# Attention and two feed-forward layers on one core: softmax's division moved behind the product, the norm's Newton steps per token, and row loads on another queue

## The chip, the cores and the metric

The program runs on one core of a Trainium2 chip. A time is the device time of one execution in microseconds; the kernel before took 961.56 us (median of three runs, 961.1 to 962.03). The profile is of one further execution of 961.0 us. In it PE is TensorE's matmuls, PEld its weight loads, DVE VectorE, ACT ScalarE, POOL GpSimd and SP the SyncE, whose queue issues nearly all DMAs.

## What is computed

The reference is a causal attention with a decay, followed by two feed-forward layers. Between the two layers, and at the end, nothing is summed over tokens, so tokens can be worked on in blocks.

```python
scores = scale * np.matmul(q, k.transpose(0, 1, 3, 2))      # batch 4, 8 heads, 576 tokens, 64 wide
cum = np.cumsum(np.log(np.clip(f, 0.0001, 1.0)), axis=-1)
scores = np.where(causal, -1000000000.0, scores + (cum[:, :, :, None] - cum[:, :, None, :]))
attn = np.exp(scores - np.max(scores, axis=-1, keepdims=True))
attn = attn / (np.sum(attn, axis=-1, keepdims=True) + 1e-09)
x = np.matmul(attn, v)                    # heads side by side: 2304 tokens x 512
y = ((x @ w1) * (x @ w2)) @ w3 @ w_out    # 512 -> 1024 -> 1024 -> 512
xn = y / np.sqrt(np.mean(y * y, axis=-1, keepdims=True) + 1e-06) * rms_g
out = (silu(xn @ w_gate) * (xn @ w_val)) @ moe2_w_out       # 512 -> 1536 -> 512
```

## The kernel before

**Attention.** 32 heads are worked on one after the other, two of them (a pair) side by side in the 128 partitions of `X`. For a head, `attn_s` multiplies queries and keys into PSUM in five blocks of query rows (`QB`; 64, 128, 128, 128 and 128 rows), `row_max` takes each block through DVE (mask, maximum, copy into `PB`), and `row_exp` makes the exponentials on ACT, with their row sums in `rsum`. `attn_t` transposes the probabilities on PE, splits them into a high part `PTh` (ACT) and a low part `PTl` (DVE), and `pv` multiplies both with the values; its last step adds the two halves into `X` (L541). The decay enters as extra rows of the product: four rows of `rq`/`rk` or `Q2`/`K2` hold 8 times the cumulated logarithm `cum` in two parts, and ones.

**Division.** For the first two pairs (heads 0 to 3) the probabilities stay undivided; `rcol`, the reciprocals of the pair spread over the columns, is transposed on PE and multiplied onto `X` (`normalize`, L543 to L556). From head 4 (`LATE`) on, `attn_s` adds 1e-9 to the five row sums, takes the reciprocals into `rinv` (L468, L469) and scales each of the five blocks of `PB` with them, on whichever of ACT, DVE and POOL is planned free first (L470 to L473).

**Rows.** `cum` of all heads is written to DRAM once (`cq_d`, `cn_d`); each later head loads its two pairs of rows from there into `Q2` and `K2` (L398, L399), issued from ACT's queue through `send`. Head 0's rows are made by DVE and ACT (L1073, L1075), head 1's by two DMAs on ACT's queue (L1083, L1084).

**First layer.** Tokens go in six blocks of 384 (`bk`). `ab_group` makes the two products of a block, L691 multiplies them, `y_group` multiplies by the product of w3 and w_out that was made beside attention (L647). `norm` then sums the squares over channels on PE with a matrix of ones, which leaves the sum in all 128 partitions, and takes the inverse root on 128x384 by a bit trick and three Newton steps (L727 to L733; the squares on ACT). The result is scaled into `yn_d`. `norm` of a block stands after the second pair of groups of the next one.

**Second layer.** Its products go through sums of weight pieces. `widen` loads a piece (1 MB), repairs its bits (L571 to L574), combines parts (L770) and stores it (`sw_d`, `wo_d`). `EARLY` = 12 pieces are planned into the first half (`raw_w`), six behind it (`xf`). `gate` (L872) and `wout` (L953) follow as one dense row of matmuls, three times.

**What sets the order.** All instructions are given to `Plan` with their durations and dependences; `begins` works out when each must start, and `order` then writes one list for each engine, in which an instruction that may run on several engines goes to the one that is planned to finish it first. Every engine runs its list in order, and SP and ACT wait in order before they issue a DMA. First-layer blocks serve as filler for PE during attention. The lines below are the functions that the change touches and what calls them.

Of the kernel before, what the change touches and what calls it, by code (L numbers as in the profile page):

```python
# [39 lines left out]
EARLY = 12  # L40
# [4 lines left out]
FROWS = D + 4  # L45
LATE = 4
# [37 lines left out]
class Plan:  # L84
# [37 lines left out]
    def begins(self):  # L122
# [4 lines left out]
        for i in range(len(ops) - 1, -1, -1):  # L127
# [12 lines left out]
    def order(self):  # L140
# [27 lines left out]
        while len(out) < n:  # L168
# [48 lines left out]
def body(ctx, tc, q, k, v, f, w12, w3, wo1, wgv, wo2, g, out):  # L217
# [166 lines left out]
    def prep(h, at):  # L384
        p = h % 2
        if h < NQ:

# [831 lines left out]
```

## Time and profile before

| | |
|---|---|
| median of three runs | 961.56 us (961.1 to 962.03) |
| the profiled execution | 961.0 us, span 959.2 us |
| PE, PEld busy | 938.5 us (98 %), 893.6 us (93 %) |
| DVE busy | 844.1 us (88 %) |
| ACT, POOL busy | 549.4 us (57 %), 231.7 us (24 %) |
| DMA on SP's and ACT's queue | 154.02 MB, 0.58 MB |
| chain that ended last | PE 63 %, DVE 27 %, issue 4 %, DMA 3 % |

A matmul counts as busy until its last result is out, and the next one begins before that; so a busy PE can still be waiting, and the weight loads (PEld) show it better. The shares are means over the whole program, whose parts have different limits; the windows below part them.

### The profile page before, as it was taken

How to read it: one execution, taken by the hardware profiler on the slowest of the kernel's cores; microseconds unless marked ns; L12 is line 12 of the kernel's file. 1: busy time of each engine (PE TensorE's matmuls, PEld its weight loads, DVE VectorE, ACT ScalarE, POOL GpSimd, SP SyncE). 2: the span in 40 equal slices, each digit the busy share in tenths (PEclk: the TensorE clock that was granted, in tenths of full speed). 3: DMA queues.
4: the chain of work that ended last, by engine and by line, in shares of the span. 5: the costliest groups of instructions: out<-in, count | busy, mean ns of one | idle time of the engine just before them, and what ended most of it. 6: DMA issues, size and time to landing. Idle time of an engine off the chain costs nothing.

```text
span 959.2 us, 15426 instructions
## 1 busy us (share of the span) xinstructions
PE 938.5 (98%) x5480; PEld 893.6 (93%) x5480; DVE 844.1 (88%) x1553; ACT 549.4 (57%) x1132; POOL 231.7 (24%) x242
## 2 busy tenths in 40 slices
PE   7999999999999999999999999999999999999998
PEld 4687889899899999899999999999999999999998
DVE  6999999999999999866666659999988899988896
ACT  4888888777776667543333244546444456454442
POOL 2145437264444442401102022015000012000000
PEclk9999999999999999999999999999999999999999
DMA  7764564645444733354864223632663334643322
GB/s 250 206 205 149 162 227 143 213 142 194 163 135 161 247 135 109 129 202 160 321 243 154 94 97 123 236 138 67 191 242 116 111 99 146 214 151 116 132 66 99
DMA packets 43868, 155.58 MB, mean 162 GB/s; under 512 B 4880, under 2 KB 20496, under 8 KB 37136
## 3 DMA queue, kind: packets, MB, share of 16 engines
q1 hardware_dynamic: 43448, 154.02, 47.4%
q8 instruction: 43, 0.70, 0.3%
q10 hardware_dynamic: 344, 0.58, 0.2%
q14 instruction: 33, 0.27, 0.1%
HBM read 124.13 MB, written 30.44 MB: 161 GB/s over the span
## 4 chain that ended last, share of the span: by engine, by line
PE 63%; DVE 27%; issue 4%; DMA 3%; ACT 2%; POOL 1%; ACTq 0%; DVEq 0%; POOLq 0%
PE bank L872 27%; PE bank L684 13%; PE bank L953 8%; PE bank L708 6%; DVE PTl L497 3%; PE wide L953 3%; DVE qk L251 3%; DVE wbig L251 1%; DVE x L541 1%; PE bank L490 1%; DVE raw_w L574 1%; PE wide L530 1%; DVE lbig L251 1%; DVE raw_w L770 1%; DVE PB4b L433 1%
## 5 line engine op out<-in xcount | busy, mean ns | idle before, releaser
L684 PE MATMUL bank<-xhl,wbig 128*128 128x384 f32 x1152 | 216.9, 338 | 0.1
L684 PEld LDWEIGHTS bank<-xhl,wbig 128*128 128x128 f32 x1152 | 198.2, 188 | 1.9 <-DVE wbig L251 0.5
L872 PE MATMUL bank<-xop,wbig 128*128 128x384 f32 x1008 | 182.6, 336 | 0.8 <-ACT cs L894 0.8
L872 PEld LDWEIGHTS bank<-xop,wbig 128*128 128x128 f32 x1008 | 175.3, 188 | 1.4 <-ACT cs L894 1.1
L872 PE MATMUL bank<-xop,lbig 128*128 128x384 f32 x504 | 95.0, 336 | 0.0
L872 PEld LDWEIGHTS bank<-xop,lbig 128*128 128x128 f32 x504 | 88.0, 188 | 0.0
L497 DVE TENSOR_TENSOR PTl<-bank,PTh 128x512 fp32r<-128x512 f32 (+3 forms) x116 | 64.6, 580 | 3.9 <-ACT PTh L496 3.5
L708 PE MATMUL bank<-uh,Wch 128*128 128x384 f32 x192 | 65.0, 339 | 0.0
L708 PE MATMUL bank<-uh,Wcl 128*128 128x384 f32 x192 | 64.4, 335 | 0.0
L708 PE MATMUL bank<-ul,Wch 128*128 128x384 f32 x192 | 64.3, 335 | 0.0
L496 ACT CAST PTh<-bank 128x512 fp32r<-128x512 f32 (+3 forms) x116 | 54.5, 506 | 11.6 <-PE bank L490 10.6
L647 PE MATMUL bank<-wbig,w 128*128 128x512 f32 x192 | 54.3, 407 | 0.0
L692 ACT CAST uh<-u 128x384 fp32r<-128x384 f32 x48 | 24.6, 514 | 43.3 <-DVE u L691 43.0
L260 POOL TENSOR_SCALAR qk<-rq 64x576 fp32r<-64x576 f32 x42 | 32.1, 769 | 58.9 <-PE wide L416 52.1
L530 PE MATMUL wide<-PTh,V 128*128 128x512 f32 (+4 forms) x145 | 45.0, 317 | 1.3 <-DVE nmaxb L433 1.1
L530 PE MATMUL wide<-PTl,V 128*128 128x512 f32 (+4 forms) x145 | 44.6, 332 | 1.0 <-DVE PTl L497 0.9
L691 DVE TENSOR_TENSOR u<-bank,a 128x384 f32<-128x384 f32 x48 | 26.4, 551 | 21.3 <-PE bank L684 21.0
L251 DVE TENSOR_TENSOR lbig<-zf,lbig 128x768 fp32r<-128x768 f32 x46 | 44.7, 978 | 0.2
L878 DVE TENSOR_TENSOR zf<-cs 128x384 f32<-128x384 f32 x72 | 39.9, 555 | 4.7 <-ACT cs L883 2.9
L251 DVE TENSOR_TENSOR wbig<-nrm,wbig 128x768 fp32r<-128x768 f32 (+1 forms) x41 | 42.9, 1047 | 0.4 <-ACT wbig L258 0.3
L258 ACT ACTIVATE lbig<-zf 128x768 fp32r<-128x768 f32 x32 | 27.2, 849 | 25.9 <-PE bank L953 9.6
L953 PE MATMUL bank<-lbig,wbig 128*128 128x384 f32 x216 | 39.3, 334 | 0.0
(329 smaller groups left out, 2283.2 us busy)
## 6 DMA issues: line engine op xcount, KB each, us to landing
xf<-sw_d SPq DMA_DIRECT2D x24, 896.0 KB
raw_w<-in_wgv SPq DMA_DIRECT2D x12, 1024.0 KB
sw_d<-raw_w SPq DMA_DIRECT2D x12, 896.0 KB
nrm<-sw_d SPq DMA_DIRECT2D x12, 896.0 KB
wbig<-w_d SPq DMA_DIRECT2D x10, 1024.0 KB
rk<-in_k SPq DMA_DIRECT2D x62, 144.0 KB
nrm<-wo_d SPq DMA_DIRECT2D x11, 768.0 KB
xf<-wo_d SPq DMA_DIRECT2D x10, 768.0 KB
```

The lines of the kernel that those rows point to most:

```text
L251: plan.op([t_dve(n, lock=True), t_pool(n)], lambda e: on[e].tensor_sub(*(x() if callable(x) else x for x in (o, a, b_))), r, w)
L258: A.activation(o_, a_, AF.Copy, scale=by)
L260: on[e].tensor_scalar(out=o_, in0=a_, scalar1=by, scalar2=1.0, op0=ALU.mult, op1=ALU.mult)
L496: act(n, lambda: A.copy(PTh[:, pt:pt + n], o[:, lo:lo + n]), [], [("PTh", pt), key], at, 55)
L497: dve(n, lambda: V.tensor_sub(PTl[:, pt:pt + n], o[:, lo:lo + n], f32(PTh[:, pt:pt + n])), [("PTh", pt)], [("PTl", pt), key], at)
L530: pe(w, lambda s_=s_, o=o, w=w, c=c, kb=kb, m=m, src=src: T.matmul(t[:, o:o + w], V2[p][:, kb, :], src[:, c:c + w], start=(s_ == 0 and m = ...
L647: T.matmul(o, a, b_, start=(ft == 0 and m == 0), stop=(ft == KF - 1 and m == 2))
L684: T.matmul(o, a, x[:, kt, :], start=(kt == 0 and i == 0), stop=(kt == KD - 1 and i == 2))
L708: T.matmul(o, a[:, es], x[:, ft, 0:w], start=(q == 0 and ft % 2 == 0 and i == 0), stop=(q == 3 and ft % 2 == 1 and i == 2))
L872: T.matmul(o, w[:, a, j, kt], x[c][:, kt], start=start and kt == 0 and i == 0, stop=kt == 1 and i == 2, skip_group_check=not start)
L878: plan.op([t_dve(TH, lock=True), t_pool(TH)], lambda e: on[e].tensor_mul(o(), x(), y()), r, w)
L953: T.matmul(tiles[m], wv[:, a, k, m], z[c][:, kt], start=start and k == 0 and x == 0, stop=k == KH - 1 and x == 2, skip_group_check=not start)
```

## The change

The probabilities of all heads stay undivided. After a pair's second head, PE transposes the 10 columns of row sums to 10 rows, DVE adds 1e-9 and takes the reciprocals (`rrow`), and SP writes them to DRAM (`r_d`) and reads them back twice, each row set spread over 64 partitions (`rall`); `normalize` multiplies `X` by it, on DVE or POOL. `norm` sums each token's squares into one column per 128 tokens, so that the Newton steps work on 128x3 (`tok`); `scale`, two pairs of groups later, transposes them, writes them to DRAM (`n_d`), reads them back over all partitions and scales. The rows of heads 0 and 1 are both made by engines, for which `f` gets 112 rows. Row loads go through SP. `EARLY` is 8, and the planner's start time of DMA and its own constant for ACT's DMAs change.

```diff
-EARLY = 12
+EARLY = 8
...
-FROWS = D + 4
-LATE = 4
+FROWS = 112
...
-DMA0, COLD, SENT, RS, RB = 4000, 7000, 2600, 230, 330
+DMA0, COLD, RS, RB = 2500, 7000, 230, 330
...
-                send(lambda: A.dma_start(out=rq[p][D:D + 2, :], in_=cq_d[h]), ["cdq"], [("nrowq", p)])
-                send(lambda: A.dma_start(out=rk[p][D + 2:D + 4, :], in_=cn_d[h]), ["cdn"], [("nrown", p), ("rk", p, 1)])
+                dma(4600, lambda: SP.dma_start(out=rq[p][D:D + 2, :], in_=cq_d[h]), ["cdq"], [("nrowq", p)])
+                dma(4600, lambda: SP.dma_start(out=rk[p][D + 2:D + 4, :], in_=cn_d[h]), ["cdn"], [("nrown", p), ("rk", p, 1)])
...
-        send(lambda: A.dma_start(out=f32(Q2[D:D + 2, :]), in_=cq_d[h]), ["cdq", "rows"], ["rowq"])
-        send(lambda: A.dma_start(out=f32(K2[D + 2:D + 4, :]), in_=cn_d[h]), ["cdn", "rows"], ["rown"])
+        dma(4600, lambda: SP.dma_start(out=f32(Q2[D:D + 2, :]), in_=cq_d[h]), ["cdq", "rows"], ["rowq"])
+        dma(4600, lambda: SP.dma_start(out=f32(K2[D + 2:D + 4, :]), in_=cn_d[h]), ["cdn", "rows"], ["rown"])
...
-        pr = h // 2 % 2
-        if h >= LATE:
-            sums, inv = rsum[pr][:, p], rinv[pr][:, p]
-            dve(10, lambda: V.tensor_scalar_add(inv, sums, 1.0e-9), [("rsum", pr, p, i) for i in range(5)], [("rinv", pr, p)], at)
-            dve(80, lambda: V.reciprocal(inv, inv), [], [("rinv", pr, p)], at)
-            for i in (1, 2, 3, 4, 0):
-                n, cols = QB[i][1], QEND[i]
-                o = PB[p][i][:n, 0:cols]
-                copy(cols, o, o, [("rinv", pr, p)], [("PB", p, i)], rinv[pr][:n, p, i:i + 1])
-        elif p:
-            dve(450, lambda: V.tensor_scalar_add(rinv[pr], rsum[pr], 1.0e-9), [("rsum", pr, j, i) for j in range(2) for i in range(5)], [("rinv", pr)], at)
-            dve(165, lambda: V.reciprocal(rinv[pr], rinv[pr]), [], [("rinv", pr)], at)
-            src = rinv[pr].rearrange("p j i -> p i j").unsqueeze(3).broadcast_to([P, 5, 2, D])
-            copy(5 * P, rcol.rearrange("p i (j d) -> p i j d", j=2), src, [("rinv", pr)], ["rcol"])
...
+        if len(parts) == 3 and p:
+            pr = h // 2 % 2
+            row, r_o = o[0:10, 3 * P:4 * P], r_d[h // 2]
+            pe(128, lambda: T.transpose(row, rsum[pr].rearrange("p j i -> p (j i)"), ident), [("rsum", pr, j, i) for j in range(2) for i in range(5)], [key], at)
+            dve(P, lambda: V.tensor_scalar_add(rrow, row, 1.0e-9), [], ["rrow", key], at)
+            dve(P, lambda: V.reciprocal(rrow, rrow), [], ["rrow"], at)
+            dma(5e3, lambda: SP.dma_start(out=r_o.rearrange("j (i n) -> (j i) n", i=5), in_=rrow), ["rrow"], [("rd", h // 2)])
+            for j in range(2):
+                dma(147e3, lambda j=j: SP.dma_start(out=rall[j * D:(j + 1) * D, :], in_=r_o[j, 0:S].partition_broadcast(D)), [("rd", h // 2)], [("rall", j)])
...
-        (b, pp), pr = divmod(h // 2, H // 2), h // 2 % 2
-        t, wk = wide, ["wide"]
-        def run():
-            for i in range(5):
-                o = (i - 1) % 5 * P
-                T.transpose(t[:, o:o + P], rcol[:, i, :], ident)
+        b, pp = divmod(h // 2, H // 2)
         x = X[b % 2][:, pp, :]
-        pe(128, run, ["rcol"], wk, at, 5)
-        dve(S, lambda: V.tensor_mul(x, x, t[:, 0:S]), [], wk + [("x", b % 2, pp, j) for j in range(2)], at)
+        plan.op([t_dve(S, lock=True), t_pool(S)], lambda e: on[e].tensor_mul(x, x, rall), [("rall", 0), ("rall", 1)], [("x", b % 2, pp, j) for j in range(2)])
...
-        n, w = mm_next(), EDGE[bk + 1] - EDGE[bk]
-        o = bank[n][:, 0:w]
-        y_sb, ms, t, r = nv[:, 0:KD, 0:w], nv[:, KD, 0:w], nv[:, KD + 1, 0:w], nv[:, KD + 2, 0:w]
-        pe(w, lambda: T.matmul(o, ones, ms, start=True, stop=True), ["acc"], [("bank", n)], clock[0], 4)
-        tick(4 * (13.4 + 0.4167 * w))
-        dve(w, lambda: V.tensor_scalar_add(ms, o, 1.0e-6), [("bank", n)], ["acc"])
-        dve(w, lambda: V.tensor_scalar(out=u32(t), in0=u32(ms), scalar1=1, scalar2=None, op0=ALU.logical_shift_right), ["acc"], ["nt0"], rate=.53, lock=True)
-        dve(w, lambda: V.tensor_scalar(out=u32(r), in0=u32(t), scalar1=-1.0, scalar2=float(0x5F3759DF), op0=ALU.mult, op1=ALU.add), ["nt0"], ["r"], rate=.53, lock=True)
+        n = mm_next() if bk < last else 4
+        o, ms = bank[n][:, 0:c], nv[:, KD, 0:BW]
+        def sums():
+            for i in range(c):
+                T.matmul(o[:, i:i + 1], ms[:, i * P:(i + 1) * P], ones[:, 0:1], start=True, stop=True)
+        pe(128, sums, ["acc"], [("bank", n)], clock[0], 2 * c)
+        tick(220 * c)
+        dve(c, lambda: V.tensor_scalar_add(m_, o, 1.0e-6), [], [("bank", n), "tok"])
+        dve(c, lambda: V.tensor_scalar(out=u32(t_), in0=u32(m_), scalar1=1, scalar2=None, op0=ALU.logical_shift_right), [], ["tok"])
+        dve(c, lambda: V.tensor_scalar(out=u32(r_), in0=u32(t_), scalar1=-1.0, scalar2=float(0x5F3759DF), op0=ALU.mult, op1=ALU.add), [], ["tok"])
         for _ in range(3):
-            act(w, lambda: A.activation(t, r, AF.Square), ["r"], ["nt0"])
-            dve(w, lambda: V.scalar_tensor_tensor(out=t, in0=t, scalar=-0.5, in1=ms, op0=ALU.mult, op1=ALU.mult), ["acc"], ["nt0"], lock=True)
-            dve(w, lambda: V.scalar_tensor_tensor(out=r, in0=t, scalar=1.5, in1=r, op0=ALU.add, op1=ALU.mult), ["nt0"], ["r"], lock=True)
+            dve(c, lambda: V.tensor_mul(t_, r_, r_), [], ["tok"])
+            dve(c, lambda: V.scalar_tensor_tensor(out=t_, in0=t_, scalar=-0.5, in1=m_, op0=ALU.mult, op1=ALU.mult), [], ["tok"])
+            dve(c, lambda: V.scalar_tensor_tensor(out=r_, in0=t_, scalar=1.5, in1=r_, op0=ALU.add, op1=ALU.mult), [], ["tok"])
+    def scale(bk):
+        n, w = mm_next() if bk < last else 5, BW
+        row = bank[n][0:c, 0:P]
+        y_sb, r = nv[:, 0:KD, 0:w], nv[:, KD + 2, 0:w]
+        pe(128, lambda: T.transpose(row, r_, ident), ["tok"], [("bank", n)], clock[0])
+        dve(P, lambda: V.tensor_copy(trow[0:c], row), [], ["trow", ("bank", n)])
+        dma(2e3, lambda: SP.dma_start(out=n_d[bk].rearrange("(i n) -> i n", i=c), in_=trow[0:c]), ["trow"], [("nd", bk)])
+        dma(512.0 * w, lambda: SP.dma_start(out=r, in_=n_d[bk].partition_broadcast(P)), [("nd", bk)], ["r"])
...
-            if h % 2 == 0 and h <= LATE:
+            if h % 2 == 0:
...
-        hi, lo, r4 = cqx[:, 0, :], cqx[:, 1, :], slice(D, D + 4)
-        e = [ident[r4, D + i:D + i + 1] for i in range(2)]
-        c = rows_c[r4, :]
-        def picks():
-            V.tensor_scalar_mul(c[:, 0:1], e[0], 8.0)
-            V.tensor_scalar_mul(c[:, 1:2], e[1], -8.0)
-        dve(100, picks, ["ident"], ["picks"], -100)
-        dve(S + 250, lambda: V.tensor_scalar(out=rq[0][r4, :], in0=cum[r4], scalar1=c[:, 0:1], scalar2=e[1], op0=ALU.mult, op1=ALU.add),
-            ["cum", "ident", "picks"], [("nrowq", 0)])
-        act(S, lambda: A.activation(rk[0][r4, :], cum[r4], AF.Identity, scale=c[:, 1:2], bias=e[0]),
-            ["cum", "ident", "picks"], [("nrown", 0), ("rk", 0, 1)])
+        hi, lo = cqx[:, 0, :], cqx[:, 1, :]
+        def first_rows(h):
+            r = slice(D + 32 * h, D + 32 * h + 4)
+            e = [ident[r, r.start + i:r.start + i + 1] for i in range(2)]
+            c = rows_c[r, :]
+            def picks():
+                V.tensor_scalar_mul(c[:, 0:1], e[0], 8.0)
+                V.tensor_scalar_mul(c[:, 1:2], e[1], -8.0)
+            dve(100, picks, ["ident"], ["picks"])
+            dve(S + 250, lambda: V.tensor_scalar(out=rq[h][r, :], in0=cum[r], scalar1=c[:, 0:1], scalar2=e[1], op0=ALU.mult, op1=ALU.add),
+                ["cum", "ident", "picks"], [("nrowq", h)])
+            act(S, lambda: A.activation(rk[h][r, :], cum[r], AF.Identity, scale=c[:, 1:2], bias=e[0]),
+                ["cum", "ident", "picks"], [("nrown", h), ("rk", h, 1)])
+        for h in range(NQ):
+            first_rows(h)
...
-        send(lambda: A.dma_start(out=rq[1][D:D + 2, :], in_=cq[1:2]), ["cq"], [("nrowq", 1)])
-        send(lambda: A.dma_start(out=rk[1][D + 2:D + 4, :], in_=cn[1:2]), ["cn"], [("nrown", 1), ("rk", 1, 1)])
-        send(lambda: A.dma_start(out=cq_d, in_=cq), ["cq"], ["cdq"])
-        send(lambda: A.dma_start(out=cn_d, in_=cn), ["cn"], ["cdn"])
+        dma(150e3, lambda: SP.dma_start(out=cq_d, in_=cq), ["cq"], ["cdq"])
+        dma(150e3, lambda: SP.dma_start(out=cn_d, in_=cn), ["cn"], ["cdn"])
...
+                if bk and n == 3 and m == 1:
+                    scale(bk - 1)
...
+    scale(last)
...
-        "f": np.concatenate([f.reshape(NH, S)] * 2 + [f.reshape(NH, S)[0:1]] * 4),
+        "f": f.reshape(NH, S)[[*range(NH)] * 2 + [0] * 32 + [1] * 16],
```

What the change moves in the order stands at three places. On ACT at the start, ahead of the first exponentials: in the old order ACT issues four DMAs (rows of head 1, then all rows to DRAM) between the table load and the first weight repair.

```order
L1075 ACTIVATE rk_98<-tmp,ident,rows_c 4x576
L1077 ACTIVATE x_126<-tmp 68x576
L1079 ACT_TABLE_LOAD
L1079 ACTIVATE rows_c<-rows_c 128x1
L1083 DMA rq_97<-x_126 2x1x576
L1085 DMA cq_d<-x_126 32x1152
L1084 DMA rk_99<-x_127 2x1x576
L1086 DMA cn_d<-x_127 32x1152
L571 ACTIVATE nrm<-nrm 128x1024
```

And the same place in the new order.

```order
L1072 ACTIVATE rk_102<-tmp,ident,rows_c 4x576
L1077 ACTIVATE x_129<-tmp 112x576
L1072 ACTIVATE rk_103<-tmp,ident,rows_c 4x576
L1079 ACT_TABLE_LOAD
L1079 ACTIVATE rows_c<-rows_c 128x1
L549 ACTIVATE nrm<-nrm 128x1024
```

The four DMAs are gone from ACT, and a second row instruction (`rk_103`, head 1) stands behind the one of head 0.

On DVE near the end of attention, in the old order: a head's high and low parts (`PTl`), the reciprocal of another head, three of its five scalings, and the addition into `X`.

```order
L497 TENSOR_TENSOR PTl<-bank_60,PTh 128x320
L468 TENSOR_SCALAR rinvb<-rsumb 128x5
L469 RECIPROCAL rinvb<-rinvb 128x5
L497 TENSOR_TENSOR PTl<-bank_61,PTh 128x384
L260 TENSOR_SCALAR PB4b<-PB4b,rinvb 128x576
L260 TENSOR_SCALAR PB2b<-PB2b,rinvb 128x320
L260 TENSOR_SCALAR PB0b<-PB0b,rinvb 64x64
L541 TENSOR_TENSOR x_127<-wide,rq_96 64x576
```

And near it in the new order.

```order
L531 TENSOR_TENSOR x_130<-wide,rq_100 64x576
L487 TENSOR_TENSOR PTl<-bank_59,PTh 128x512
L478 TENSOR_SCALAR rrow<-bank_61 10x128
L479 RECIPROCAL rrow<-rrow 10x128
L487 TENSOR_TENSOR PTl<-bank_60,PTh 128x448
L487 TENSOR_TENSOR PTl<-bank_61,PTh 128x320
L487 TENSOR_TENSOR PTl<-bank_59,PTh 128x384
```

The scalings are gone; one addition and one reciprocal on 10 partitions stand for both heads of the pair.

On SP late in attention, in the old order: the loads of keys, queries and values, a store of a weight piece (`sw_d`) and a load of the next (`raw_w`).

```order
L378 DMA rk_99<-in_k 64x576
L375 DMA rq_97<-in_q 64x576
L376 DMA rk_99<-in_k 64x576
L794 DMA sw_d<-raw_w_1294 128x1792
L382 DMA rv_101<-in_v 128x320
L562 DMA raw_w_1294<-in_wgv 128x2048
```

And a like place in the new order.

```order
L378 DMA rv_104<-in_v 128x320
L789 DMA sw_d<-raw_w_1282 128x1792
L394 DMA qk_106<-cq_d 2x576
L395 DMA qk_106<-cn_d 2x576
L609 DMA wbig<-w_d 128x2048
L374 DMA rk_103<-in_k 64x576
L371 DMA rq_101<-in_q 64x576
L372 DMA rk_103<-in_k 64x576
L480 DMA r_d<-rrow 10x128
L540 DMA raw_w_1282<-in_wgv 128x2048
L378 DMA rv_105<-in_v 128x320
L482 DMA rall<-r_d 64x576 x2
```

A head's row loads (L394, L395) now stand in SP's line, here right behind a store, and the pair's reciprocals go out (L480) and come back (L482) in the same line.

## Rows read from the trace of the kernel before

**Rows 1.** Windows: stretch, length; busy us (instructions) per engine; clock, DMA share, GB/s.
```profile
0.00:20.00 20.00, 14.93 (x36) 7.36 (x36) 14.77 (x34) 9.06 (x18) 4.98 (x26) 1.00 0.78 241
20.00:40.00 20.00, 18.60 (x92) 13.27 (x91) 17.01 (x39) 16.15 (x36) 2.32 (x3) 0.91 0.71 220
40.00:380.00 340.00, 331.83 (x2048) 304.10 (x2047) 333.09 (x764) 262.45 (x621) 152.68 (x168) 1.00 0.52 171
380.00:420.00 40.00, 37.95 (x234) 35.49 (x233) 32.71 (x71) 20.16 (x47) 10.82 (x12) 1.00 0.43 151
420.00:560.00 140.00, 140.00 (x806) 139.47 (x805) 89.20 (x150) 46.22 (x82) 21.87 (x20) 1.00 0.54 193
```

**Rows 2.** PEld's waits from 20 to 420 us: us in total, times, longest.
```profile
PEld wide L530 <- DVE PTl L497: 3.2, 7, 0.8
PEld bank L490 <- DVE nmaxb L433: 3.1, 6, 1.1
...
PEld bank L490 <- DVE PB2b L260: 0.3, 1, 0.3
```

**Rows 3.** The chain of waits in order of time: start us, us, what.
```profile
196.73 1.20 PE bank L490 x11
...
318.03 4.72 DMA raw_w<-in_wgv
...
459.58 8.32 PE bank L684 x48
468.54 24.96 PE bank L684 x144
...
560.71 4.16 PE bank L872 x24
```

**Rows 4.** Windows of the tiles rinva, then rinvb: DVE, ACT, POOL, as above.
```profile
0.00:420.00 420.00, 24.33 (x67) 15.18 (x31) 1.84 (x3) 1.00 0.53 175
0.00:420.00 420.00, 25.45 (x65) 14.91 (x32) 2.93 (x4) 1.00 0.53 175
```

**Rows 5.** Single lines: ns min/median/max, first and last start us, forms.
```profile
L541 DVE TENSOR_TENSOR x<-wide,rq x29: 749/750/753, 61.8 to 419.2; 64x576 f32<-64x576 f32 x29
L468 DVE TENSOR_SCALAR rinvb<-rsumb x14: 149/155/170, 79.5 to 402.0; 128x5 f32<-128x5 f32 x14
L469 DVE RECIPROCAL rinva<-rinva x14: 170/174/191, 58.4 to 375.1; 128x5 f32<-128x5 f32 x14
L476 DVE RECIPROCAL rinva<-rinva x1: 203/203/203, 30.5 to 30.5; 128x10 f32<-128x10 f32 x1
```

**Rows 6.** Single lines of the norm.
```profile
L728 DVE TENSOR_SCALAR nrm<-nrm x6: 321/353/360, 251.2 to 571.3; 128x384 uint32<-128x384 uint32 x6
L732 DVE SCALAR_TENSOR_TENSOR nrm<-nrm x18: 507/551/559, 267.6 to 590.0; 128x384 f32<-128x384 f32 x18
```

**Rows 7.** The tile raw_w from 170 to 440 us, two of its lines.
```profile
L770 DVE TENSOR_TENSOR raw_w<-raw_w x29: 374/420/1227, 216.3 to 436.1; 128x256 f32<-128x256 f32 x29
...
L574 DVE SCALAR_TENSOR_TENSOR raw_w<-raw_w x13: 1208/1220/1693, 178.4 to 432.7; 128x1024 uint32<-128x1024 uint32 x13
```

**Rows 8.** SP's timeline from 440 to 500 us: start us, us, what.
```profile
440.17 0.96 SPq L562 DMA_DIRECT2D xf<-in_wo  x2
...
499.21 0.52 SPq L796 DMA_DIRECT2D wo_d<-xf  x1
```

**Rows 9.** Timeline of the start.
```profile
13.54 0.61 ACTq L1084 DMA_DIRECT2D rk<-x  x1
...
19.42 3.42 PE L414 MATMUL bank<-rk,rq 128*128 128x448 f32 x8 [2.73 <-DMA qk<-cq_d]
```

**Rows 10.** Timeline from 242.5 to 249 us.
```profile
243.69 0.23 ACTq L399 DMA_DIRECT2D qk<-cn_d  x1
...
248.09 0.36 PE L416 MATMUL bank<-qk 128*128 128x448 f32 x1
```

**Rows 11.** SP's waits over the whole program: us in total, times, longest.
```profile
SPq L794 <- DVE raw_w L770: 36.3, 8, 12.7
```

More of the change, by code (lines that the diff above doesn't have):

```diff
@@ L97, in __init__ @@
         self.groups, self.group = {}, ""
-        self.sent = set()
     def op(self, alts, fn, r=(), w=(), at=None):
@@ L130, in begins @@
             t = by[i] - ns - self.LAG[e]
-            if e == "SP" or i in self.sent:
+            if e == "SP":
                 t -= 2250
@@ L198, in order @@
                 free[e], done = t + 550, dma + 1700
-            elif i in self.sent:
-                free[e], done = t + ns, t + ns + SENT
             else:
@@ L282, in body @@
     wo_d = dram.tile([P, NOP, KH, 256], F32, name="wo_d")
+    r_d = dram.tile([NH // 2, 2, 5 * P], F32, name="r_d")
+    n_d = dram.tile([NT // BW, BW], F32, name="n_d")
     right = ExitStack()
@@ L296, in body @@
     g_sb = const.tile([P, KD], F32, name="g_sb")
+    tok = const.tile([P, 3 * BW // P], F32, name="tok")
+    trow = const.tile([BW // P, P], F32, name="trow")
     rq = [att.tile([P, S], F32, name=f"rq{i}") for i in range(2)]
@@ L311, in body @@
     rsum = [att.tile([P, 2, 5], F32, name=f"rsum{t}") for t in "ab"]
-    rinv = [att.tile([P, 2, 5], F32, name=f"rinv{t}") for t in "ab"]
-    rcol = att.tile([P, 5, P], F32, name="rcol")
+    rrow = att.tile([10, P], F32, name="rrow")
+    rall = att.tile([P, S], F32, name="rall")
     mask = att.tile([P, S], F32, name="mask")
@@ L693, in ab_group @@
             sub(w, lambda: ul()[:, fb, 0:w], u, lambda: f32(uh()[:, fb, 0:w]), [("u", fb % 2), ("uh", fb)], [("ul", fb)] + [("raw", "ul")] * first)
+    last = len(EDGE) - 2
     nv = nrm.rearrange("p (k n) -> p k n", k=7)
@@ L719, in y_group @@
         group("left")
+    c = BW // P
+    m_, t_, r_ = (tok[:, i * c:(i + 1) * c] for i in range(3))
     def norm(bk):
-        n, w = mm_next(), EDGE[bk + 1] - EDGE[bk]
-        o = bank[n][:, 0:w]
-        y_sb, ms, t, r = nv[:, 0:KD, 0:w], nv[:, KD, 0:w], nv[:, KD + 1, 0:w], nv[:, KD + 2, 0:w]
-        pe(w, lambda: T.matmul(o, ones, ms, start=True, stop=True), ["acc"], [("bank", n)], clock[0], 4)
-        tick(4 * (13.4 + 0.4167 * w))
-        dve(w, lambda: V.tensor_scalar_add(ms, o, 1.0e-6), [("bank", n)], ["acc"])
@@ L1049, in start @@
         for p in range(2):
-            dve(S, lambda p=p: (V.memset(rq[p][D:P, :], 0.0), V.memset(rk[p][D:P, :], float(p)), p and V.memset(rq[p][D:D + 4, :], 1.0)), w=[("nrowq", p), ("nrown", p), ("rk", p, 1)])
+            dve(S, lambda p=p: (V.memset(rq[p][D:P, :], 0.0), V.memset(rk[p][D:P, :], 0.0)), w=[("nrowq", p), ("nrown", p), ("rk", p, 1)])
         for i in range(WARM):
@@ L1106, in body @@
             wc_group(i, WC0 + i * WCP, WCP)
-    last = len(EDGE) - 2
     need = [(e - 1) // S for e in EDGE[1:]]
```

5 lines of the change are left out of this document (1 added, 4 removed).

## The prediction

> **What bounds the kernel now.** Three views, in this order. First the windows [rows 1], whose five numbers are the busy time of PE, PEld, DVE, ACT and POOL. The program has two halves. From 40 to 380 us, attention with the first feed-forward blocks as filler, DVE is busy 333.09 of 340 us, while PE is not dense: its weight loads take only 304.10 us. From 420 to 560 us it is the reverse: PE 140.00 of 140, PEld 139.47, DVE 89.20. So VectorE holds the first half and TensorE the second. TensorE's granted clock is 1.00 in both, its upper level of 2.4 GHz.
>
> Second, who made TensorE wait in the first half: the waits of PEld from 20 to 420 us [rows 2]. Fourteen rows of that answer name a DVE instruction, the first 3.2 us, the last 0.3 us, together 20.1 us; eleven others (ACT, POOL, "issue") make 9.6 us. The DVE rows are the most that a lighter VectorE can give back in this half.
>
> Third, the chain of waits [rows 3], for PE's own prices: 48 matmuls of 128x384 took 8.32 us, 173 ns each; 11 transposes took 1.20 us, 109 ns each; and between the end of the 48 at 467.90 and the next piece at 468.54 stands one norm's sum over channels, 0.64 us. In the chain the gate's products begin at 560.71; the last addition of attention, L541, begins at 419.2 [rows 5]. Between the two PE has only dense work.
>
> Since the work behind attention is dense and stays, every us of stall that leaves the first half comes off the end, and no more than that. The rest is how many.
>
> **The change part by part.**
>
> *Division after the product.* Removed for heads 4 to 31: a head's addition, reciprocal and five scaling copies. Everything on the two tiles of reciprocals [rows 4] is 24.33 + 25.45 = 49.8 us of DVE, 30.1 us of ACT, 4.8 us of POOL. Added per pair of heads, 16 times: on PE one transpose (109 ns, 1.7 us in all); on DVE an addition and a reciprocal over 10x128 and a 576-wide multiplication; three DMAs. The addition of 5 columns took 155 ns, so I take 0.2; the multiplication is near L541's 0.75 [rows 5], and the order gives DVE 10 of the 16, POOL 6. No row has a reciprocal of 128 columns: 5 columns took 174 ns, 10 took 203 ns [rows 5]. At 5.8 ns per further column it would be 0.89 us; the lower bound is the addition's 0.2. I take 0.89. Back for DVE: 16 x (0.2 + 0.89) + 10 x 0.75 = 24.9 us; 25 us gained, up to 36 with the short reciprocal.
>
> *Norm.* Six times. On DVE before: the sum out of PSUM, twice 0.353 and six steps of about 0.55 [rows 6], 4.6 us with 0.55 for the sum, and three squares on ACT. After: 12 instructions of 128x3 and one row copy, each near 0.155 us as the 5-column addition is, 2.0 us. By the order three norms stand ahead of the end of attention, as before: 3 x 2.6 = 8 us of DVE. PE: six sums of 0.64 us go, 3.8 us; six times three one-column products of two passes and a transpose come, at 109 ns 4.6 us. The scaling's wait for its two DMAs lies between the second and the fourth pair of groups of the next block: 48 matmuls, 8.3 us of cover. Uncovered, it would hold only the write of yn_d, which nothing needs for tens of us.
>
> *EARLY 12 to 8.* Four weight pieces leave the first half. Each has a shift of 1.22 us, one of about half that, and combinations of 0.42 us [rows 7] on DVE, 3 to 4 us; by the order one of the twelve stood behind the end of attention already, so 12 us leave. In the second half DVE has 140 - 89.2 = 50.8 us idle from 420 to 560 us [rows 1]. There the question is time: before, six pieces took from 440.17 to 499.21 [rows 8], 9.8 us each, so ten take 98 us. They can begin when attention ends, the load of x and its first operand follow within some 10 us, and the gate begins 141 us after the end of attention. Margin some 30 us: I cost it at nothing. Beyond the margin each us would be a us of PE.
>
> *First rows by engines.* Head 1's rows came by DMA: rk<-x was issued at 13.54 us, and the PE matmul that needs it began at 19.42 after 2.73 us idle [rows 9]. Now engines make them beside head 0's. At most 2.7 us on PE, at least 0, as VectorE has older work queued there; I take 2.
>
> *Row loads from ACT's queue to SP's.* 62 DMAs move, two go, and 60 come (r_d, rall, n_d, nrm). SP issues in order: a row load waits until the head before has left Q2, and behind it stand the next q, k and v loads. Before, the second row of a head went out at 243.69 us and the head's first matmul began at 248.09 [rows 10]: 4.4 us of slack, in one of the short gaps. On SP's queue a row may stand behind a weight load of 1 MB, which took 4.72 us [rows 3]; by the order about ten heads have one right ahead. Bounds: 0, since PE has filler, and 10 x 4.72 = 47 us. The weight loads are mostly issued while the head before still runs, so I take 1.5.
>
> The Trainium skill, "DMA: Bandwidth & Descriptors", section "Issuing engines are not separate DMA queues", says that DMAs of all issuing engines run on the same 16 engines and interleave, so that another issuer saves issue time only; by that rule the move costs nothing and the sum is 947. Its section "Queues, rings and completion order" says that SP and ACT have a ring each and that an engine takes a ring's descriptors in order; by that a row now stands behind a load that it could pass before, and the sum goes towards the 47 us. The row at the start, with 5.9 us from issue to use on ACT's queue while SP's loads ran, fits the first; no run here yet shows the second.
>
> *Sum.* DVE work ahead of the end of attention falls by 25 + 8 + 12 = 45 us, from 397.6 us (four windows of rows 1) to about 353, 11 %. Taking 45 us off the 419 us would put the end of attention at 374; but PE, with all its DVE waits and the 2.7 us at the start gone, ends it at 419.2 - 20.1 - 2.7 = 396. So PE becomes the bound, with DVE at 353 / 400 = 88 %. At that load some waits stay, since PE takes its instructions in order; of the 20.1 us I take two thirds, 13.4. With PE's work (1.7 + 4.6 - 3.8, and ten transposes of the first pairs gone, 1.1: +1.4): -13.4 - 2 + 1.4 + 1.5 = -12.5. The profiled execution took 961.0 us (span 959.2), 0.56 under the median of 961.56. 961.0 - 12.5 = 948.5.
>
> **The rivals.**
> *All the waits go.* If VectorE always runs ahead: 961.0 - 20.1 - 2.7 + 1.4 = 940. For it: DVE is the releaser in most of the rows. Against it: maximum, exponential, transpose and product follow each other in any case.
>
> *The pair's reciprocals arrive late.* A block can begin only when its batch's x is multiplied. Before, that was after the last addition; now two DMAs in a row, write and read back, stand behind the last head's sums. The blocks that follow the ends of batches 0, 1 and 2 wait for that; batch 3's is covered, as its first block stands at 459.58 [rows 3], 40 us after attention. A small DMA was done within the 4.4 us of [rows 10]; of two in a row half runs beside the head's transposes and product: 3 x 4.4 = 13 us, which gives 961.5, no change. For it: SP stands still between write and read. Against it: the sums are ready before the transposes begin.
>
> *SP's line.* SP waits for the combinations before it stores a weight piece: L794 36.3 us in 8 waits behind DVE, the longest 12.7 [rows 11]. That harmed no row while rows had another queue. Now all eight early stores stand ahead of some row load. If a head's first matmul slips by 1 us at each of 30 heads, it is 30 us: 978.5, slower. It decides from 12.5 / 30 = 0.42 us per head.
>
> **How the numbers follow.** The forecast 0.62, with its own range 942 to 955. All waits go, 0.10. Late reciprocals, 0.15. SP's line, 0.13. Faster by over 0.2 % (1.9 us, about what a measurement of this kernel can tell from no change) are the first two and 0.06 of the third, 0.78; within 0.2 % 0.08 of the third; slower the last and 0.01, 0.14. The range, 938 to 961, leaves out SP's line and the edges of the others.
>
> **What would show it.** Right: DVE about 300 of 340 us from 40 to 380, PEld's DVE waits near 7 us, PE's dense stretch some 12 us earlier and as long as before, head 1's first matmul near 17 us. Wrong: PE or PEld waiting for a row load in many heads; PE idle ahead of a block's first product behind x<-x,rall; PE idle ahead of the gate behind xop. If DVE stays near 98 %, the 45 us are the step that failed.

## The result, and the profile after

The changed kernel takes 951.39 us (median of 4 runs, 951.07 to 951.89) against 961.79 for the kernel before on the same chip (4 runs, 961.10 to 962.46): 10.4 us less, ratio 0.9892 with the interval 0.9875 to 0.9909. The forecast was 948.5, 12.5 less. The profiled execution's span is 949.3 us (before 959.2).

The windows of the kernel after, as [rows 1]; the five busy times are PE, PEld, DVE, ACT and POOL:

```profile
0.00:20.00 20.00, 17.83 (x50) 9.64 (x51) 15.73 (x43) 12.13 (x24) 6.78 (x27) 1.00 0.73 253
20.00:40.00 20.00, 17.89 (x99) 12.81 (x97) 19.88 (x38) 16.24 (x36) 2.00 (x3) 1.00 0.87 265
40.00:380.00 340.00, 333.78 (x2088) 309.14 (x2089) 319.11 (x695) 237.92 (x573) 152.87 (x167) 1.00 0.55 181
380.00:420.00 40.00, 40.00 (x254) 39.44 (x253) 21.40 (x54) 16.19 (x34) 6.20 (x7) 1.00 0.33 119
420.00:560.00 140.00, 140.00 (x816) 139.82 (x815) 89.84 (x169) 45.81 (x78) 22.29 (x24) 1.00 0.60 214
```

From 40 to 380 us DVE is busy 319.11 us, 14 fewer than before, where the forecast had 300. PE's share rises by only 2 us, but its weight loads by 5 and its matmuls from 2048 to 2088. Attention ends sooner. This is the line of its last addition, as the first of [rows 5] (ns min/median/max, first and last start us):

```profile
L531 DVE TENSOR_TENSOR x<-wide,rq x29: 748/750/752, 59.5 to 407.2; 64x576 f32<-64x576 f32 x29
```

It starts last at 407.2 instead of 419.2, 12 us earlier. From there to the gate's products the chain of waits, as [rows 3] (start us, us, what), is TensorE alone:

```profile
407.06 8.44 PE bank L662 x48
...
448.89 8.32 PE bank L662 x48
457.77 9.47 PE bank L662 x54
467.36 15.61 PE bank L662 x90
...
533.67 16.64 PE bank L687 x96
550.32 6.24 PE bank L867 x36
```

The first of these answers to a row of the kernel before:

```profile
417.98 24.96 PE bank L684 x144
```

The block that began at 459.58 begins at 448.89 (-10.7), the gate at 550.32 instead of 560.71 (-10.4), and the time ends 10.4 lower. The 12 us are those of VectorE's last addition. TensorE's dense run behind its last products begins at 407.06 instead of 417.98, 10.9 us earlier, so of its own gain only some 0.5 us are given back behind the attention. The gate begins as the piece before it ends (533.67 + 16.64 = 550.31), so no weight piece holds it up. The norm stands in the gaps of this chain: 0.56 us between the first two lines (its sums) and 0.12 behind the second (the transpose of its row), where the old sum took 0.64.

The waits of PEld from 20 to 420 us, as [rows 2], begin so after the change:

```profile
PEld wide L520 <- DVE PTl L487: 4.5, 7, 1.5
PEld bank L471 <- DVE nmaxb L429: 2.9, 3, 1.4
PEld bank L471 <- DVE nmaxa L429: 2.9, 5, 0.9
```

All rows of it that name DVE make 15.3 us (before 20.1), those that name another engine or "issue" 6.9 (before 9.6).

Where the gain lies shows in finer windows. Before, and then after:

```profile
20.00:100.00 80.00, 75.45 (x417) 59.53 (x416) 76.40 (x182) 67.25 (x154) 29.08 (x40) 0.98 0.62 196
100.00:180.00 80.00, 78.40 (x462) 69.77 (x461) 79.26 (x161) 66.69 (x149) 41.25 (x38) 1.00 0.51 172
180.00:300.00 120.00, 117.89 (x761) 112.48 (x760) 118.12 (x281) 88.65 (x221) 52.02 (x59) 1.00 0.52 173
300.00:405.00 105.00, 101.64 (x645) 96.57 (x643) 99.88 (x235) 69.72 (x173) 41.64 (x44) 1.00 0.44 151
```

```profile
20.00:100.00 80.00, 75.48 (x426) 59.11 (x425) 79.02 (x173) 61.01 (x146) 33.72 (x41) 1.00 0.65 207
100.00:180.00 80.00, 77.40 (x464) 69.69 (x464) 79.38 (x150) 60.50 (x136) 35.42 (x31) 1.00 0.58 190
180.00:300.00 120.00, 118.79 (x781) 115.28 (x781) 109.44 (x248) 83.11 (x205) 55.37 (x61) 1.00 0.54 182
300.00:405.00 105.00, 105.00 (x683) 102.40 (x682) 82.63 (x190) 59.92 (x147) 36.55 (x43) 1.00 0.41 139
```

Up to 180 us DVE is as full as before (79.02 and 79.38 of 80) and TensorE's weight loads stand where they stood, with 11 matmuls more. Little was freed there: from 20 to 180 us the old division held DVE for 18.7 us (by windows of the tiles, rinva 9.92, rinvb 6.52 and rcol 0.80, and two multiplications, 1.5) and the new one holds it for 10.3 (rrow 7.23, the multiplications 3.04), and other work took the place of the 8.4. From 180 to 405 us the old one held 33.3, the new one 16.6. Only behind 180 us does DVE have room (109.44 of 120, 82.63 of 105), and there TensorE runs 20 and 38 matmuls more in the same time. The price that the prediction could only bound, the reciprocal of 128 columns, stands in one line of the kernel after:

```profile
L479 DVE RECIPROCAL rrow<-rrow x16: 929/935/941, 41.8 to 398.3; 10x128 f32<-10x128 f32 x16
```

It takes 0.935 us (0.89 estimated). The plan that orders the instructions was told `dve(P, ...)`, 70 + 1.04 x 128 = 203 ns: 16 times 0.73, 11.7 us of VectorE, are missing in it.

### The profile page after: what moved, and what is told of

It is laid out like the page before. It is cut to its first block, busy times and chain, and to the rows that moved or that the text cites. A ratio compares the mean times of both kernels' runs of the same rounds, so it can differ in the third digit from the quotient of the medians.

```text
span 949.3 us, 15520 instructions
## 1 busy us (share of the span) xinstructions
PE 934.7 (98%) x5516; PEld 894.5 (94%) x5516; DVE 814.3 (86%) x1486; ACT 516.1 (54%) x1056; POOL 227.7 (24%) x238
## 4 chain that ended last, share of the span: by engine, by line
PE 73%; DVE 12%; DMA 2%; issue 2%; ACT 0%; SPq 0%; DVEq 0%
PE bank L867 27%; PE bank L662 16%; PE bank L687 10%; PE bank L948 9%; PE wide L948 3%; PE bank L471 3%; PE wide L520 3%; DVE PTl L487 1%; DVE wbig L247 1%; DMA raw_w<-in_wgv 1%; PE bank L625 1%; DVE qk L247 1%; PE bank L413 1%; PE bank L412 1%; DVE lbig L247 1%
## 5 line engine op out<-in xcount | busy, mean ns | idle before, releaser
L486 ACT CAST PTh<-bank 128x512 fp32r<-128x512 f32 (+2 forms) x116 | 55.3, 506 | 25.9 <-PE bank L471 21.5
L487 DVE TENSOR_TENSOR PTl<-bank,PTh 128x512 fp32r<-128x512 f32 (+2 forms) x116 | 64.3, 576 | 4.7 <-ACT PTh L486 4.4
L765 POOL TENSOR_TENSOR xf<-xf 128x768 f32<-128x768 f32 (+1 forms) x5 | 23.8, 4756 | 81.7 <-DVE xf L552 25.4
L625 PEld LDWEIGHTS bank<-wbig,w 128*128 128x128 f32 x192 | 33.9, 189 | 6.6 <-DVE wbig L247 1.2
```

What stands on the lines that cost most here:

```text
L486: act(n, lambda: A.copy(PTh[:, pt:pt + n], o[:, lo:lo + n]), [], [("PTh", pt), key], at, 55)
L487: dve(n, lambda: V.tensor_sub(PTl[:, pt:pt + n], o[:, lo:lo + n], f32(PTh[:, pt:pt + n])), [("PTh", pt)], [("PTl", pt), key], at)
L625: T.matmul(o, a, b_, start=(ft == 0 and m == 0), stop=(ft == KF - 1 and m == 2))
```

## The experiments

The kernel before had medians of 961.79, 961.54 and 961.58 us in the three groups of runs. **Theory A**: what counts is VectorE's load in the attention. **Theory B** (later C, more sharply): what counts is whether the written order fits the true durations. **Theory D**: any other order lands anywhere within 5 us.

**Extra VectorE work, early and late.** 24 fills of 128x576 behind the row maxima, of which the plan knows nothing:

```
+            if 2 <= h <= 13 and i in (4, 2):      # load_late: 17 <= h <= 28
+                V.memset(dum, 0.0)
```

> The changed kernel with 24 extra DVE memsets of 576 columns (0.54 us each, on a scratch tile) beside the row maxima of heads 2 to 13, unknown to the planner, so that every engine's list is the same otherwise. 13 us more DVE work between about 25 and 165 us. Theory A (VectorE's load is what ends last up to about 180 us, where it is busy 79.0 of 80 us in the changed kernel): nearly all of it comes out at the end, 951.4 + 10 to 13 = 961 to 964. Theory B (the waits there are the chain's latency, and what counts is how the lists fit): DVE's additions shift little, 952 to 955.

> The same 24 memsets, at heads 17 to 28, about 214 to 350 us. Theory A: there DVE has 33 us idle between 180 and 405 us in the changed kernel, and PE is the bound: +0 to 3 us, 951.4 to 954.5. Theory B: as much as at the early heads, 952 to 955 for both; if both cost 10 us or more, DVE is the bound everywhere and the idle time is of no use.

Measured: load_early 962.11 (960.23 to 963.46), ratio 1.0002 [0.9990, 1.0015]; load_late 956.53, ratio 0.9944 [0.9931, 0.9956]. The fills of load_early, and two of its windows:

```profile
L433 DVE MEMSET dum<- x24: 538/538/538, 27.6 to 178.9; 128x576 f32 x24
```

```profile
20.00:100.00 80.00, 71.20 (x389) 53.51 (x388) 78.19 (x173) 57.04 (x137) 31.57 (x37) 1.00 0.63 203
100.00:180.00 80.00, 74.47 (x433) 64.89 (x431) 78.64 (x154) 58.03 (x130) 32.06 (x29) 1.00 0.54 175
```

12.9 us of fills up to 180 us cost 10.7 us, 0.8 of their time, and TensorE has 68 matmuls fewer there: theory A's number. The same from 217 us on costs 5.1, 0.4 of its time, although DVE had over 30 us idle from 180 to 405: neither theory's number. Idle time of an engine with a fixed order is only partly usable. Both runs add unplanned work, so they price load and misfit together.

**The reciprocal shortened, or only told truly.** recip_on_columns adds and inverts the sums as 128x10 columns ahead of the transpose, with ScalarE copying the row; recip_planned changes one number that only the plan reads:

```
-            pe(128, lambda: T.transpose(row, rsum[pr]..., ident), ...)
-            dve(P, lambda: V.tensor_scalar_add(rrow, row, 1.0e-9), [], ["rrow", key], at)
-            dve(P, lambda: V.reciprocal(rrow, rrow), [], ["rrow"], at)
...
+            dve(10, lambda: V.tensor_scalar_add(rinv[pr], rs, 1.0e-9), keys, [("rinv", pr)], at)      # rs: the 10 columns of sums
+            dve(120, lambda: V.reciprocal(rinv[pr], rinv[pr]), [], [("rinv", pr)], at)
+            pe(128, lambda: T.transpose(row, rinv[pr], ident), [("rinv", pr)], [key], at)
+            act(P, lambda: A.copy(rrow, row), [], ["rrow", key], at, 180)
```

```
-            dve(P, lambda: V.reciprocal(rrow, rrow), [], ["rrow"], at)
+            dve(830, lambda: V.reciprocal(rrow, rrow), [], ["rrow"], at)
```

> The changed kernel with addition and reciprocal of the pair's row sums on 128x10 (0.16 and 0.20 us) ahead of the transpose, and the transposed rows copied by ACT. DVE does 16 x (0.274 + 0.935 - 0.36) = 13.6 us less, 7 of the 16 pairs ahead of 180 us, so 6 us there. Theory A: 4 to 6 us of it come out at the end, 945.5 to 947.5. Theory B: 951 within 1.5.

> The same instructions as the changed kernel, but the planner is told 0.93 us for the reciprocal of 128 columns in place of 0.20 us, so lists are made anew. DVE's work is the same. Theory A: 950.5 to 952. Theory B: lists that know the delay save the chain's waits, 947 to 950.

Measured: recip_on_columns 950.4, ratio 0.9883 [0.9866, 0.9900]: a miss for theory A, which had 945.5 to 947.5, and within theory B's 951 +- 1.5. But this run has a stall of its own. One of its additions was held up beside GpSimd (last section), the next head's row maxima stood behind it on DVE, and TensorE stood still for 3.59 us:

```profile
31.42 0.30 PE L472 MATMUL bank<-ident,PB2b 128*128 128x128 f32 x1 [3.59 <-DVE nmaxa L430]
```

```profile
32.00:36.00 4.00, 4.00 (x18) 3.64 (x17) 3.14 (x7) 3.62 (x9) 1.27 (x1) 0.57 0.90 297
```

The second line is a window: the granted clock was 0.57 in the 4 us behind that (0.50, the lower level of 1.2 GHz, from about 32.3 to 35.7), so the stall and the slow stretch together cost some 5 us (an estimate: 3.59, and half of 3.4), and the miss alone doesn't refute theory A. recip_planned 946.57, ratio 0.9839 [0.9825, 0.9852]: as theory B has it, 4.8 us less than after with the same instructions. Its first window in the attention:

```profile
20.00:100.00 80.00, 77.74 (x451) 63.51 (x450) 78.48 (x178) 66.36 (x160) 42.30 (x50) 1.00 0.65 210
```

Against the kernel after DVE does 178 instructions for 173, ACT 160 for 146, POOL 50 for 41 in the same 80 us, and TensorE 451 matmuls for 426. A reading that fits, though no run shows it alone: a plan that believes VectorE to be free sooner than it is leaves it work that two emptier engines could have taken. Over all of 0 to 407.3 us GpSimd is busier than in the kernel after (175.05 us for 167.85), but VectorE no less (367.69 for 366.85).

**Each part undone in the kernel after.** old_division puts back a head's reciprocals and scalings from head 4 on (`LATE = 4`, the lines that the diff removes; heads 0 to 3 as before too); early_12 sets `EARLY = 12`; old_norm puts back the old `norm` and drops `scale`; rows_by_ACT has the row loads and the two stores of rows sent by ScalarE again:

```
-                dma(4600, lambda: SP.dma_start(out=rq[p][D:D + 2, :], in_=cq_d[h]), ["cdq"], [("nrowq", p)])
+                send(lambda: A.dma_start(out=rq[p][D:D + 2, :], in_=cq_d[h]), ["cdq"], [("nrowq", p)])
...
```

> The kernel after with the old division put back (from head 4 on each head's reciprocals and five scalings of its probabilities, before the transposes); norm, EARLY and the first rows stay as changed. About +26 us of work in the attention's elementwise lists, of which some goes to ScalarE and GpSimd, so some +20 us on VectorE between 20 and 407 us. Theory A (VectorE's load sets the attention, at the rates measured here: 0.8 us of the span for a us added before 160 us, 0.4 for one added after): half of it early, half late, x 0.6 = +12, but the slow reciprocal of 128 columns, which the planner takes for five times shorter, also goes, -5: about 958 (955 to 961). Theory B (how well the order written out fits true durations sets it): with the reciprocal gone the lists fit again and the division costs little: 947 to 952.

> The kernel after with EARLY back at 12: four more raw_w groups on GpSimd with their VectorE counterparts (about +13 us on VectorE) inside the attention, and four fewer behind it. Theory A: they are placed late, where a us costs 0.4: +5, 954 to 958. Theory B: planned work finds the idle pieces (some 33 us on VectorE after 180 us): 950 to 953.

> The kernel after with the old norm put back (the sum over all 128 partitions by a matrix of ones, Newton's steps on 128x384 on VectorE and ScalarE, no row through DRAM). VectorE +4 to 5 us, on the last 110 us of the attention or behind it, TensorE about the same. Theory A: +2 (0.4 per us): 953 to 954. Theory B: within a us of after, 950.5 to 952.5. If the row's way through DRAM and the second transpose cost something, 948 to 950.

> The kernel after with the row loads of heads 2 and up issued by ScalarE's queue again, as before the change, everything else as changed. If SyncE's line (loads waiting behind the store of the reciprocals and the broadcast) delayed heads: 2 to 4 faster, 947 to 949.5. If the move was free, as the trace of after reads (heads' first matmul 4 to 9 us after the loads landed): 951.4 +-1.

Measured: old_division 963.23, ratio 1.0019 [1.0005, 1.0032]; early_12 952.03, 0.9906 [0.9888, 0.9924]; old_norm 951.76, 0.9895 [0.9876, 0.9914]; rows_by_ACT 955.95, 0.9944 [0.9924, 0.9963]. Against the 951.39 of after the division is worth 11.8 us, beyond theory A's range and far from theory B's; EARLY and the norm, 0.6 and 0.4, can't be told from nothing, as theory B had them both. Undoing the move of the rows costs 4.6 where both readings had a gain or nothing. The division's return shows from 100 us on, with 20, 25 and 18 matmuls fewer than in the kernel after:

```profile
100.00:180.00 80.00, 75.11 (x444) 66.86 (x443) 79.28 (x164) 61.43 (x136) 29.44 (x28) 1.00 0.49 162
180.00:300.00 120.00, 117.72 (x756) 111.59 (x755) 116.25 (x290) 89.65 (x220) 44.06 (x46) 1.00 0.48 159
300.00:405.00 105.00, 102.88 (x665) 99.30 (x664) 94.87 (x233) 68.35 (x172) 37.38 (x40) 1.00 0.40 135
```

The parts sum to 17.4 for a change of 10.4; each undoing makes a new order, and orders alone differ by up to 6.3 us with the same instructions, as the next runs show. The division's 11.8 is nearly twice that, the 4.6 of the rows is not beyond it. For the rows by ScalarE no single wait grew to explain 4.6: PEld's DVE waits from 20 to 420 us are 18.1 for 15.3, its ACT waits 5.2 for 4.0. One wait of PE in this run names a row load, 0.9 us. Whether ScalarE's time for issuing or the order did it stays open.

**What the plan is told.** Only the number for the reciprocal differs in told_half (400 for P) and told_long (1470 for P); true_costs has 830 there and also true numbers for the change's other small instructions; cols_true is recip_on_columns with true numbers (130 for the addition, 140 for ScalarE's copy). From true_costs:

```
-            dve(P, lambda: V.tensor_scalar_add(rrow, row, 1.0e-9), [], ["rrow", key], at)
+            dve(196, lambda: V.tensor_scalar_add(rrow, row, 1.0e-9), [], ["rrow", key], at)
...
-        dve(P, lambda: V.tensor_copy(trow[0:c], row), [], ["trow", ("bank", n)])
+        dve(196, lambda: V.tensor_copy(trow[0:c], row), [], ["trow", ("bank", n)])
-        dve(c, ...)        # six places in norm
+        dve(110, ...)
```

> The kernel after with the planner told 0.49 us for the reciprocal of a pair's sums (it takes 0.93; after tells 0.20). The program's work is the same, only the order written out differs. Theory C (what the planner is told must be true; the nearer, the better): between after (951.4) and recip_planned (946.6), 948 to 950. Theory D (any other order lands somewhere within some 5 us, recip_planned was luck): 946 to 956, no order among the three.

> The kernel after with the planner told 1.60 us for the reciprocal, 0.67 too long. Theory C: as wrong as after in the other direction, 949 to 952; it wastes VectorE's time in the plan but leads to no wait, so no worse than after. Theory D: 946 to 956.

> recip_planned with the other small instructions of the change told as they ran too: the pair's addition 0.27 us (told 0.20), the copy of the norm's row 0.27 (told 0.20), the norm's steps on 128x3 0.18 (told 0.07). Theory C: at or below recip_planned, 944 to 947. Theory D: 946 to 956.

> recip_on_columns (950.4: the addition and the reciprocal of a pair on 128x10, before its transpose) with the planner told 0.21 us for the addition (told 0.08 there) and 0.22 for ScalarE's copy of the row (it ran 0.25). VectorE has some 12 us less to do than in recip_planned. Theory A and C together: below recip_planned, 941 to 945. Theory D: 946 to 956; if what counts is that the addition on columns waits for five exponentials at the head of VectorE's list (2.3 us at 25 us in recip_on_columns), about 950 again.

Measured, with all waits of PEld behind DVE from 20 to 420 us added up:

| kernel | told, us (runs 0.93) | time, us | ratio to before | PEld behind DVE, us |
|---|---|---|---|---|
| after | 0.20 | 951.39 | 0.9892 [0.9875, 0.9909] | 15.3 |
| told_half | 0.49 | 949.26 | 0.9874 [0.9851, 0.9896] | 12.8 |
| recip_planned | 0.93 | 946.57 | 0.9839 [0.9825, 0.9852] | 9.8 |
| told_long | 1.60 | 949.47 | 0.9875 [0.9855, 0.9894] | 10.3 |
| true_costs | 0.93, others too | 945.12 | 0.9835 [0.9811, 0.9860] | 7.9 |
| cols_true | 0.20 on columns, where it runs 0.21 | 948.87 | 0.9876 [0.9852, 0.9899] | 10.2 |

The medians fall towards the true number and rise beyond it: theory C's order. The intervals carry less: only recip_planned and true_costs stand clear of after, those of told_half and told_long overlap it. With one order for each number theory D, too, is unlikely rather than excluded (true_costs alone lies outside its 946 to 956). Nor do the waits of the last column give the time by themselves: recip_on_columns has 7.5 us of them at 950.4, as PEld's part of its long stall is put to "issue" (3.9 us). true_costs is the fastest of all, 16.5 us under before and 6.3 under the change as made; over recip_planned its interval doesn't set it apart. Its windows up to 180 us:

```profile
20.00:100.00 80.00, 77.46 (x448) 63.19 (x447) 78.57 (x178) 66.29 (x160) 38.45 (x51) 1.00 0.66 211
100.00:180.00 80.00, 78.45 (x483) 73.14 (x482) 79.47 (x153) 59.75 (x132) 48.83 (x31) 1.00 0.59 202
```

DVE is as full as after the change (78.57 and 79.47 of 80), yet TensorE has 41 matmuls more in the two: a VectorE as full, with another order. cols_true missed the 941 to 945 that A and C had together, without such a stall. What it lost, it lost early, as in

```profile
20.00:100.00 80.00, 74.54 (x418) 58.49 (x417) 78.61 (x172) 62.01 (x150) 32.25 (x43) 1.00 0.69 212
```

30 matmuls fewer than true_costs, while from 180 to 300 us PE is busy 120.00 of 120. The long first addition that its expectation names doesn't return: at 23.9 us it takes 0.16. In recip_on_columns it took 2.40, beside GpSimd (below), and not for want of exponentials. Three rows of PEld's waits from 20 to 100 us are 2.9 us longer than in true_costs (PTl 2.9 for 1.2, nmaxa 1.5 for 0.9 and 0.8 for 0.2). Why that order is poor ahead of 100 us is open, and so is what 12 us less of planned VectorE work are worth by themselves.

## Why the prediction was right, and where not

The direction was right, and the end near the forecast (-10.4 for -12.5). That the size came near is in part luck: the main term of the sum came out at about a third, and others that the sum didn't have made up for it.

*Head 1's rows*: forecast -2, at most 2.7. The start came at the upper end, -2.7: the row that answers to the 19.42 of [rows 9] is

```profile
16.69 2.23 PE L410 MATMUL bank<-rk,rq 128*128 128x448 f32 x8
```

But more went than the gap. In the kernel before the same eight matmuls took 3.42 us: TensorE had stood still for 2.73 us, and 0.9 us after it went on its granted clock fell. The same stretch, before and then after:

```profile
20.30:23.70 3.40, 3.40 (x10) 2.55 (x10) 1.79 (x8) 1.94 (x4) 0.21 (x1) 0.50 0.89 297
20.30:23.70 3.40, 2.29 (x15) 1.40 (x14) 3.34 (x8) 3.19 (x10) 0.00 (x0) 1.00 0.46 103
```

It was 0.50, the lower level of 1.2 GHz, for 3.4 us, which is 1.7 us lost, and the prediction had no term for that although [rows 1] shows 0.91 from 20 to 40 us. Executions differ in it: in the first group of runs the kernel before took 958.93 and 959.27 us where its mean granted clock was 1.000, and 960.88 to 964.93 in the thirteen others (0.996 to 0.998; less clearly so in the other two groups); all four executions of the kernel after had 0.999 or 1.000.

*VectorE's work, -45 us*: this is the step that failed. Its parts were sized well as durations. Up to the end of attention the scalings (38.3 us), the reciprocals with their additions (14.8) and two old multiplications (1.5) go, and reciprocals of rows (15.0), additions (4.4) and multiplications (7.5) come: -28 for -25; raw_w -12.8 for -12; the norm -9.6 + 5.3, -4.3 for -8, as the steps of two norms, not three, ran ahead of that end. All durations of VectorE together fall from 454.3 to 413.1, -41. Busy time falls from 396.9 to 366.9, only -30:

```profile
0.00:419.30 419.30, 402.62 (x2399) 359.51 (x2400) 396.91 (x905) 307.82 (x722) 170.80 (x207) 1.00 0.53 175
```

```profile
0.00:407.30 407.30, 396.80 (x2412) 358.42 (x2413) 366.85 (x802) 277.35 (x657) 167.85 (x201) 1.00 0.55 180
```

The first is the kernel before, the second after. In the records neighbours on VectorE overlap. In the timeline of the kernel before two scalings read

```profile
260.47 0.51 DVE L260 TENSOR_SCALAR PB4a<-PB4a,rinva 128x576 f32<-128x576 f32 x1
260.90 0.45 DVE L260 TENSOR_SCALAR PB3a<-PB3a,rinva 128x448 f32<-128x448 f32 x1
```

The first is recorded with 0.51 us and the next begins 0.43 after it. 103 instructions went; at 0.08 each that is 8 of the 11 us between -41 and -30. A count times a mean duration overstates what short instructions give back.

*Two thirds of the DVE waits, -13.4*: they fell by 4.8, from 20.1 to 15.3. The rule of thumb assumed that room on VectorE is spread evenly and that the written order uses it. Neither holds: up to 180 us there is no room, and the order was made with a reciprocal 4.6 times too short. With the true number (recip_planned) the waits fall to 9.8 and with all of them (true_costs) to 7.9, near the 7 that the forecast had. The gain of the kernel after is larger than these waits: other waits of PEld fell by 2.7, the start gave 2.7 and the clock at the start 1.7. With the 4.8 that makes 11.9, or 10.8 without 1.1 of the other waits that stand in the slow stretch itself and would count twice; TensorE's dense run begins 10.9 earlier. It's no exact account, since TensorE's own work changed too.

*PE becomes the bound with DVE at 88 %*: true behind 180 us only, where from the windows above DVE is at 109.44 + 82.63 = 192.07 of 225, 85 %, with PE at 223.79; ahead of it DVE is at 99 %.

*EARLY and the norm*: the prediction gave them 20 of the 45 us; the runs, 0.6 and 0.4 us of time, none that can be told from nothing. *The division*: 25 of the 45, and without it no gain is left (old_division 963.23, no faster than before).

*Row loads on SP's queue*, +1.5, and the rival *SP's line*, 978.5: both fell. SP waits, but for what a head needs anyway, and for the store of the reciprocals:

```profile
SPq L394 <- PE wide L413: 60.1, 25, 5.9
SPq L480 <- DVE rrow L479: 37.9, 11, 20.8
```

No wait of PE or PEld names a row load in the kernel after (in other orders some do, at most 1.0 us each: told_half, load_late, cols_true), and undoing the move makes it slower (955.95), the other sign. By the Trainium skill, "DMA: Bandwidth & Descriptors", "Issuing engines are not separate DMA queues", the move should change issue time only; that no wait for a row appeared agrees, and the 4.6 us of rows_by_ACT it neither shows nor excludes. By the section "Queues, rings and completion order" of the same page of the Trainium skill an engine takes a ring's descriptors in order, which would have gone towards 47 us; no run shows such a delay.

*The pair's reciprocals late*, 961.5: fell. No wait of TensorE names the multiplied x; the one wait behind it that the trace has is 1.1 us on ACT.

## What to carry to other kernels

Work taken from a busy engine came off the end here only where no other work took its place, and work added where that engine had idle time still cost 0.4 of its length. Ask by stretches, not over the whole, where the work goes. Where a planner writes the order, an instruction that is new to it must be measured and its cost told before the change is judged: here that one number was worth 4.8 us, beside 10.4 for the change itself. A gap of TensorE at the start cost more than its length here, since the clock fell behind it. Size a removal by busy time with and without, not by counts times mean durations.

## What the runs showed of the hardware

VectorE's reciprocal follows its columns: 174 ns for 128x5, 203 for 128x10 [rows 5], 935 for 10x128, so 118 further columns took 732 ns, 6.2 ns each, close to the 5.8 from 5 to 10 columns; no run has the same number of columns on 10 and on 128 partitions. Very small instructions are dear: three columns took 158 to 166 ns in the median in all six lines of the norm's steps after the change, two of them shown (ns min/median/max), and 128 columns out of PSUM 274.

```profile
L478 DVE TENSOR_SCALAR rrow<-bank x16: 268/274/279, 29.5 to 398.0; 10x128 f32<-10x128 f32 x16
L717 DVE TENSOR_TENSOR tok<-tok x18: 145/162/165, 240.0 to 564.6; 128x3 f32<-128x3 f32 x18
L718 DVE SCALAR_TENSOR_TENSOR tok<-tok x18: 146/158/730, 241.7 to 565.1; 128x3 f32<-128x3 f32 x18
```

In recip_on_columns one addition of 128x10, 158 ns in the median, took 2.40 us and ended with a subtraction that GpSimd had begun 0.51 us before it:

```profile
24.80 2.88 POOL L247 TENSOR_TENSOR wbig<-raw_ul,wbig 128x1024 fp32r<-128x1024 f32 x1 [4.81 <-DVE wbig L256]
25.31 2.40 DVE L480 TENSOR_SCALAR rinva<-rsuma 128x10 f32<-128x10 f32 x1
```

The Trainium skill, "SBUF — State Buffer", section "SBUF: two separate sides", says that GpSimd and VectorE share a pair of ports, and that an instruction of GpSimd and one of VectorE in a two-port mode (or with two inputs in SBUF) exclude each other for the whole of an instruction, whichever starts first; these two rows agree, but they don't show the addition's mode, and no run here tests it alone. The plan's cost for that addition has no such exclusion (`lock`).
